# A long-convolution transform factored 64x64 in place of 256x16, with 32x64 and 64x32 array tiles in its first and last stage

## Chip, cores and metric

The kernel runs on one core of one Trainium2 chip. The metric is device time in microseconds (us) of one execution. A stage time is read from a single execution, and one difference of less than about 6 us in it is not firm. An execution of more than 1.5% above the fastest of its kernel is called slow and is left out of ratios. Where a profile is quoted, it is one execution, and its span is about 2 us shorter than the time that goes with it.

## The reference, cut to what matters

```python
def _A_ref(q, k, v, shift_k, ssm_k, ssm_D):        # H3: S = 2048 rows, D = 1024 channels
    k_shift = sum(k_pad[:, t:t+S, :] * shift_k[:, ks-1-t] for t in range(4))
    kv = k_shift * v
    y = irfft(rfft(kv, 2*S) * rfft(ssm_k, 2*S))[:S]  # causal convolution of length 4096
    return q * (y + kv * ssm_D)
def _B_ref(x, Lambda, B, C, log_dt, Dskip):         # S5: complex diagonal scan along S
    ...                                             # cut
    return 2 * Re(C h) + x * Dskip
return concatenate([a, b], axis=-1)                 # bfloat16, 2048 x 2048
```

Half A is the part that the change touches. One warning for what follows: evaluated on its inputs, the reference has values of about 3.8e-7 rms in half A and 2.5e-3 rms in half B. The comparison of outputs therefore does not see half A at all.

## The kernel before

Half A is a discrete Fourier transform of 4096 points, cut into factors, in three stages with scratch in DRAM between them. Stage 1 loads k and v, forms kv, transforms along the partitions and stores `Ys_kv` and `Ys_h`. Stage 2 loads those, multiplies the spectra, transforms back along the other factor and stores `Vs`. Stage 3 loads `Vs` as `vv`, does the last transform, multiplies by q and stores. Half B, in 16 chunks, runs beside all three, and a planner fixes one order of instructions for each engine.

```python
N1, N2, NFFT = 256, 16, 4096
kr = k.rearrange("(n s) d -> n s d", s=N2)           # vr, qr, oar alike: row t = 16*p + s
...
def k_(r):
    t_ = st["kring"][:, (r + 3) % c["kr"], :]        # a ring of buffers
    eng = spd if r > 0 else gpd                      # SyncE's hardware queue / GpSimd's queue
    if r >= 0:
        eng(t_, kr[:, r, :])                         # 128 partitions, 2 KB each
...
def am(n2, w):                                       # stage 1: 4 matmuls of 128x128 per n2
    cc, dh = divmod(w, 2)
    st["pa", n2, w] = ptile("ps_a", [P, 512])
    nc.tensor.matmul(st["pa", n2, w][:], F1t[:, cc, :], st["kv", n2][:, dh * 512:(dh + 1) * 512], start=True, stop=True)
...
E["ast"] = lambda n2, w: gpd(Ys_kv[w, n2, :, :], st.pop(("ysb", n2, w))[:])
...
def vl(n2):                                          # stage 3
    st["vv", n2] = atile("a3", "vv", [P, 2, D])
    for cc in range(2):
        spd(st["vv", n2][:, cc, :], Vs[cc, n2, :, :])
def ql(n2):
    st["qt", n2] = atile("a3", "qt", [P, D])
    spd(st["qt", n2][:], qr[:, n2, :])
def a3_(n2, w):
    ...
    for cc in range(2):
        nc.tensor.matmul(pt[:], Gt[:, cc, :], st["vv", n2][:, cc, w * 512:(w + 1) * 512], start=(cc == 0), stop=(cc == 1))
...
E["ost"] = lambda n2: gpd(oar[:, n2, :], st.pop(("ot", n2))[:])
```

## Time and profile before

The time is 401.72 us, the median of 3 runs (401.33 to 404.17). The stages end where the next one's first load is issued, which makes a table:

| border, before | us from the start |
|---|---|
| last k load issued | 125.2 |
| first l2h load issued (stage 1 ends) | 176.3 |
| first vv load issued (stage 2 ends) | 339.2 |
| end | 401.5 |

So the stages take 176.3, 162.9 and 62.3 us. The borders come from the views of single tiles. A line of such a view gives the issuing line, the engine, the output and input, the count, the shortest, median and longest issue in ns, and the time of the first and last issue:

```profile
L664 SPq DMA_DIRECT2D kring<-in_A_k_dram x15: 328/437/4037, 9.4 to 125.2; - x15
L764 SPq DMA_DIRECT2D l2h<-Ys_h x16: 339/498/1605, 176.3 to 305.2; - x16
```

The page's rows of 40 slices (one slice is 10 us here) show where the transfers were dense; a digit is the mean busy share of 16 DMA engines in tenths:

```profile
DMA  6999799698888463468599994998698553999982
GB/s 181 278 270 303 254 309 326 194 358 308 284 287 234 137 221 97 157 175 327 133 318 289 326 293 61 305 320 282 214 335 270 185 145 144 338 368 330 335 282 106
```

Until 130 us and again from 340 us most slices stand at 8 or 9 (10 of 13, and 5 of 6).

### The profile page before, as it was taken

To read this page: it belongs to the slowest core of one execution; us is meant where nothing else is said; L and a number is where in the kernel's file an instruction comes from. 1 tells how busy PE (TensorE), PEld (TensorE's weight loads), DVE (VectorE), ACT (ScalarE), POOL (GpSimd) and SP (SyncE) were. 2 spreads that over 40 slices of the span, in tenths; PEclk is the share of its full clock that TensorE was granted. 3 is DMA by queue.
4 is the path that set the end of the run, shared out by engine and by line. 5 is a ranking of instruction groups with operands and counts; after the bars stand their busy time and mean duration, and the time that the engine had idled before them with its cause. 6 is when DMAs were issued, how large, how long until landed. Compare 5 with 4: busy or idle time off the path is not lost.

```text
span 401.5 us, 9098 instructions
## 1 busy us (share of the span) xinstructions
PE 366.2 (91%) x3593; PEld 248.6 (62%) x3593; DVE 336.4 (84%) x338; ACT 291.6 (73%) x527; POOL 132.1 (33%) x228
## 2 busy tenths in 40 slices
PE   3589989998999999896989999798999999999994
PEld 0489988977668778582544465563655457667441
DVE  7695589998799999999779999984969894969861
ACT  6598989999797887642778976588778883453542
POOL 7002243435465564511333332224222431021121
PEclk9999999999999999998999999999999999999998
DMA  6999799698888463468599994998698553999982
GB/s 181 278 270 303 254 309 326 194 358 308 284 287 234 137 221 97 157 175 327 133 318 289 326 293 61 305 320 282 214 335 270 185 145 144 338 368 330 335 282 106
DMA packets 55132, 101.15 MB, mean 252 GB/s; under 512 B 23204, under 2 KB 25252, under 8 KB 55089
## 3 DMA queue, kind: packets, MB, share of 16 engines
q1 hardware_dynamic: 40864, 57.17, 47.3%
q0 software_dynamic: 14224, 43.40, 31.2%
q8 instruction: 28, 0.46, 0.5%
q14 instruction: 16, 0.12, 0.1%
HBM read 54.41 MB, written 33.55 MB: 219 GB/s over the span
## 4 chain that ended last, share of the span: by engine, by line
PE 42%; DMA 15%; issue 14%; DVE 13%; ACT 9%; POOL 4%; SPq 2%; POOLq 0%; ACTq 0%; DVEq 0%
PE ps_y L641 14%; PE ps_u L588 12%; PE ps_a L805 5%; PE ps_a L772 5%; DMA wts<-a_c_W 4%; DMA hab<-hab 3%; DVE h L618 3%; DMA Ys_kv<-ysb 3%; DVE hab L796 2%; DMA Ys_h<-ysbh 2%; DMA ld<-in_B_B_re_dram 2%; ACT ysbh L750 2%; POOL out_dram L850 2%; PE ps_a L698 1%; POOL Ys_h L757 1%
## 5 line engine op out<-in xcount | busy, mean ns | idle before, releaser
L641 PE MATMUL ps_y<-CT,h 128*128 128x512 bf16 x512 | 138.1, 381 | 3.6 <-ACT yo L656 1.6
L588 PEld LDWEIGHTS <-BT 128*128 128x128 bf16 x2048 | 120.8, 99 | 9.0 <-issue 1.5
L588 PE MATMUL ps_u<-xT,BT 128*128 128x128 bf16 x2048 | 126.0, 221 | 0.1
L641 PEld LDWEIGHTS <-h 128*128 128x128 bf16 x512 | 47.0, 98 | 50.8 <-DVE h L630 2.5
L618 DVE TENSOR_TENSOR_SCAN h<-rtab,h 128x1024 bf16<-128x1024 f32 x32 | 71.5, 2276 | 0.3
L590 ACT CAST u<-ps_u 128x512 bf16<-128x512 f32 x64 | 37.9, 604 | 41.9 <-PE ps_u L588 41.8
L757 POOL DMA_DIRECT2D Ys_h<-ysbh x64 | 46.2, 724 | 38.8 <-ACT ysbh L750 38.7
L796 DVE TENSOR_TENSOR hab<-x,hab 128x2048 bf16<-128x2048 bf16 x32 | 38.5, 1221 | 14.8 <-ACT hab L779 6.5
L600 DVE TENSOR_TENSOR mt<-u,Z 128x4096 bf16<-128x4096 bf16 x16 | 36.6, 2289 | 11.2 <-ACT u L590 11.0
L779 ACT CAST hab<-ps_a 128x512 bf16<-128x512 f32 x64 | 36.2, 600 | 10.8 <-DMA l2h<-Ys_h 5.7
L790 POOL DMA_DIRECT2D hab<-hab x32 | 16.8, 526 | 76.3 <-ACT hab L779 64.7
L817 ACT CAST vsb<-ps_a 128x512 bf16<-128x512 f32 x64 | 34.7, 596 | 9.7 <-PE ps_a L805 6.2
L785 ACT CAST x<-ps_a 128x512 bf16<-128x512 f32 x64 | 36.9, 599 | 5.2 <-PE ps_a L772 5.0
L750 ACT CAST ysbh<-ps_a 128x512 bf16<-128x512 f32 x64 | 36.8, 637 | 4.3 <-DMA Ys_h<-ysbh 2.6
L707 ACT CAST ysb<-ps_a 128x512 bf16<-128x512 f32 x64 | 36.0, 629 | 5.2 <-DMA Ys_kv<-ysb 1.6
L805 PE MATMUL ps_a<-hab,wts 128*128 128x512 bf16 x128 | 33.5, 380 | 4.0 <-DVE hab L796 3.2
L600 DVE TENSOR_TENSOR mt<-h,Z 128x4096 bf16<-128x4096 bf16 x16 | 36.5, 2283 | 0.0
L709 POOL DMA_DIRECT2D Ys_kv<-ysb x32 | 17.9, 559 | 53.4 <-ACT ysb L707 53.3
L681 DVE TENSOR_TENSOR mt<-kring,wbc 128x4096 bf16<-128x4096 bf16 (+3 forms) x16 | 30.2, 1886 | 0.1
L553 PE MATMUL ps_t<-ident,ld 128*128 128x128 bf16 x256 | 21.1, 233 | 9.2 <-DMA ld<-in_B_B_re_dram 5.8
L646 PE MATMUL ps_y<-Dd,xT 128*128 128x128 bf16 x128 | 28.0, 219 | 0.0
L772 PE MATMUL ps_a<-l2h,wts 128*128 128x512 bf16 x64 | 21.9, 386 | 5.6 <-DMA wts<-a_c_W 5.4
(117 smaller groups left out, 473.4 us busy)
## 6 DMA issues: line engine op xcount, KB each, us to landing
Ys_kv<-ysb POOLq DMA_DIRECT2D x32, 256.0 KB, 3.8
Ys_h<-ysbh POOLq DMA_DIRECT2D x64, 128.0 KB, 3.3
l2h<-Ys_h SPq DMA_DIRECT2D x16, 512.0 KB, 5.9
l2k<-Ys_kv SPq DMA_DIRECT2D x16, 512.0 KB, 8.2
hab<-hab POOLq DMA_DIRECT2D x64, 128.0 KB, 4.1
Vs<-vsb POOLq DMA_DIRECT2D x16, 512.0 KB, 7.2
vv<-Vs SPq DMA_DIRECT2D x32, 256.0 KB, 5.0
hk<-in_A_ssm_k_dram SPq DMA_DIRECT2D x8, 512.0 KB, 7.2
```

The source lines that it names most:

```text
L588: nc.tensor.matmul(pu[:, w, jl, :], BT[:, 2 * jp + jl, w, d, :], xT[:, d, :], start=(d == 0), stop=(d == ND - 1))
L590: E["ue"] = lambda i, jp: nc.scalar.copy(st["u", i][:, :, 2 * jp:2 * jp + 2, :], st.pop(("pu", i, jp))[:])
L600: nc.vector.tensor_mul(m, s_, win(Z))
L618: nc.vector.tensor_tensor_scan(gf[:, a * W:(a + 1) * W], rt1, gf[:, a * W:(a + 1) * W], 0.0, ALU.mult, ALU.add)
L641: nc.tensor.matmul(py[:], h[:, 1 - w, j, :], CT[:, j, w, dh * 512:(dh + 1) * 512], start=(j == 0 and w == 0), stop=(j == NJ - 1 and w == 1))
L750: nc.scalar.copy(st["yh", qd, n4, w // 2][:, :, w % 2, :], st.pop(("pa", qd, n4, w))[:].rearrange("p (c d) -> p c d", c=2))
L757: gpd(Ys_h[cc, n0:n0 + 2, :, qd * DQ:(qd + 1) * DQ].rearrange("n k d -> k n d"), t_[:, cc, :, :])
L772: nc.tensor.matmul(st["ps", nm, g, w][:], st["w", gq][:, gi, 0, :], st[nm, gq][:, gi, w * 512:(w + 1) * 512], start=True, stop=True)
L779: nc.scalar.copy(st["hab", g][:, 0, w * 512:(w + 1) * 512], st.pop(("ps", "l2h", g, w))[:])
L785: nc.scalar.copy(st["x16", g][:, w * 512:(w + 1) * 512], st.pop(("ps", "l2k", g, w))[:])
L796: nc.vector.tensor_mul(hab[:], st.pop(("x16", g))[:].unsqueeze(1).to_broadcast([P, 2, D]), hab[:])
L805: nc.tensor.matmul(pt[:], st["w", gq][:, gi, 1 + a, :], hab[:, a, w * 512:(w + 1) * 512], start=(a == 0), stop=(a == 1))
```

## The change

The intent is cheaper matrix work. With 64x64 factors, the first and last transforms contract over 32 and 64 rows only, so TensorE's array can be used as several small tiles side by side. To put four groups of 32 rows onto the partitions, the sequence is read in another order: row t is 64n + 16q + r, and partition 32q + n gets it. The diff, cut to its core:

```diff
-N1, N2, NFFT = 256, 16, 4096
+N1, N2, NFFT = 64, 64, 4096
...
-    kr = k.rearrange("(n s) d -> n s d", s=N2)
...                                                   (v, q and out_a alike)
+    kr, vr, qr, oar = (a.rearrange("(n q s) d -> q n s d", q=4, s=NR) for a in (k, v, q, out_a))
...
-            eng(t_, kr[:, r, :])
+            eng(t_, kr[:, :, r, :])
...
-        cc, dh = divmod(w, 2)
-        nc.tensor.matmul(..., F1t[:, cc, :], st["kv", n2][:, dh * 512:(dh + 1) * 512], start=True, stop=True)
+        b = 32 * w
+        for dh in range(2):
+            nc.tensor.matmul(pt[64 * dh:64 * dh + 64, :], F1t[b:b + 32, :], st["kv", n2][b:b + 32, dh * 512:(dh + 1) * 512], start=True, stop=True)
...
-    E["ast"] = lambda n2, w: gpd(Ys_kv[w, n2, :, :], st.pop(("ysb", n2, w))[:])
+        for dh in range(2):
+            gpd(Ys_kv[n2, 2 * w:2 * w + 2, :, dh * 512:(dh + 1) * 512].rearrange("q k d -> k q d"), t_[64 * dh:64 * dh + 64, :, :])
...
-        for cc in range(2):
-            spd(st["vv", n2][:, cc, :], Vs[cc, n2, :, :])
+        for dh in range(2):
+            spd(st["vv", n2][64 * dh:64 * dh + 64, :, :], Vs[n2, :, :, dh * 512:(dh + 1) * 512].rearrange("q k d -> k q d"))
...
-        spd(st["qt", n2][:], qr[:, n2, :])
+        spd(st["qt", n2][:], qr[:, :, n2, :])
...
-        for cc in range(2):
-            nc.tensor.matmul(pt[:], Gt[:, cc, :], st["vv", n2][:, cc, w * 512:(w + 1) * 512], start=(cc == 0), stop=(cc == 1))
+        for qt in range(4):
+            nc.tensor.matmul(pt[32 * qt:32 * qt + 32, :], Gt[64 * w:64 * w + 64, :], st["vv", n2][64 * w:64 * w + 64, qt, :],
+                             start=True, stop=True, tile_position=(64 * w, 32 * qt))
...
-    E["ost"] = lambda n2: gpd(oar[:, n2, :], st.pop(("ot", n2))[:])
+    E["ost"] = lambda n2: gpd(oar[:, :, n2, :], st.pop(("ot", n2))[:])
```

In what follows, a "narrow" transfer is one whose DRAM side is [4, 32, 1024], and a "wide" one has at least 32 rows as its slowest dimension.

More of the change, by code (lines that the diff above doesn't have):

```diff
@@ L20 @@
 TWO_PI = 2.0 * math.pi
-N1, N2, NFFT = 256, 16, 4096
+N1, N2, NFFT = 64, 64, 4096
 NG = 32
+NR = 16
 def a_constants():
-    n1 = np.arange(128)[:, None]; k1 = np.arange(128)[None, :]
+    n1 = np.arange(32)[:, None]; k1 = np.arange(NG)[None, :]
     ang = 2 * np.pi * n1 * (k1 + 0.5) / N1
-    F1 = np.stack([np.cos(ang), -np.sin(ang)], axis=1)
-    G = np.stack([np.cos(ang.T) * 2 / NFFT, -np.sin(ang.T) * 2 / NFFT], axis=1)
-    s = np.arange(4)[:, None, None, None]; g = np.arange(NG)[None, :, None, None]
-    n2 = np.arange(N2)[None, None, :, None]; k2 = np.arange(N2)[None, None, None, :]
-    kk1 = 32 * s + g
-    phi = 2 * np.pi * n2 * (2 * kk1 + 1 + 2 * N1 * k2) / (2 * NFFT)
-    cph, sph = np.cos(phi), np.sin(phi)
-    W2 = np.zeros((2, 4, N2, NG, 2, 4, N2))
-    Wa = np.zeros((2, 4, N2, NG, 2, 4, N2))
-    Wb = np.zeros((2, 4, N2, NG, 2, 4, N2))
-    for si in range(4):
-        c_ = cph[si]; s_ = sph[si]
-        c_n2k2 = np.transpose(c_, (1, 0, 2)); s_n2k2 = np.transpose(s_, (1, 0, 2))
-        W2[0, si, :, :, 0, si, :] = c_n2k2
-        W2[1, si, :, :, 0, si, :] = s_n2k2
-        W2[0, si, :, :, 1, si, :] = -s_n2k2
-        W2[1, si, :, :, 1, si, :] = c_n2k2
-        c_k2n2 = np.transpose(c_, (2, 0, 1)); s_k2n2 = np.transpose(s_, (2, 0, 1))
-        Wa[0, si, :, :, 0, si, :] = c_k2n2
-        Wa[0, si, :, :, 1, si, :] = s_k2n2
-        Wa[1, si, :, :, 0, si, :] = -c_k2n2
-        Wa[1, si, :, :, 1, si, :] = -s_k2n2
-        Wb[0, si, :, :, 0, si, :] = -s_k2n2
-        Wb[0, si, :, :, 1, si, :] = c_k2n2
-        Wb[1, si, :, :, 0, si, :] = -s_k2n2
-        Wb[1, si, :, :, 1, si, :] = c_k2n2
-    f = lambda a: np.ascontiguousarray(a.reshape(128, -1), dtype=np.float32).astype(ml_dtypes.bfloat16)
-    W2 = np.transpose(W2, (0, 2, 1, 3, 4, 5, 6))
-    Wa = np.transpose(Wa, (0, 1, 2, 3, 4, 6, 5))
-    Wb = np.transpose(Wb, (0, 1, 2, 3, 4, 6, 5))
-    W3 = np.stack([W2.reshape(128, NG, 128), Wa.reshape(128, NG, 128), Wb.reshape(128, NG, 128)], axis=2)
-    return f(F1), f(G), f(W3)
@@ new lines, in a_constants @@
+    f1 = np.stack([np.cos(ang), -np.sin(ang)], axis=1).reshape(32, 64)
+    F1 = np.tile(f1, (4, 1))
+    F1h = np.zeros((32, 4, 2, 2, 64))
+    for qt in range(4):
+        F1h[:, qt, qt // 2, qt % 2, :] = f1
+    G = np.tile(np.concatenate([np.cos(ang.T), -np.sin(ang.T)], axis=0) * 2 / NFFT, (2, 1))
+    r = np.arange(NR)[:, None]; qt = np.arange(4)[None, :]
+    n2 = (16 * qt + r).reshape(-1)[:, None, None]
+    g = np.arange(NG)[None, :, None]
+    k2 = np.arange(N2)[None, None, :]
+    phi = 2 * np.pi * n2 * (2 * g + 1 + 2 * N1 * k2) / (2 * NFFT)
@@ new lines, in a_constants @@
+    co, si = np.cos(phi), np.sin(phi)
+    W2 = np.stack([np.stack([co, -si], axis=2), np.stack([si, co], axis=2)], axis=1)
+    cT, sT = (np.transpose(a, (2, 1, 0)) for a in (co, si))
+    Wa = np.stack([np.stack([cT, sT], axis=3), np.stack([-cT, -sT], axis=3)], axis=0)
+    Wb = np.stack([np.stack([-sT, cT], axis=3), np.stack([-sT, cT], axis=3)], axis=0)
+    f = lambda a: np.ascontiguousarray(a.reshape(128, -1), dtype=np.float32).astype(ml_dtypes.bfloat16)
+    W3 = np.stack([a.reshape(128, NG, 128) for a in (W2, Wa, Wb)], axis=2)
@@ L63 @@
+    return f(F1), f(F1h), f(G), f(W3)
 class Task:
@@ L344, in full_kernel @@
     Dd = const.tile([P, ND, P], BF16, name="Dd")
-    F1n, Gn, W3n = a_constants()
+    F1n, Fhn, Gn, W3n = a_constants()
     F1d = nc.inline_tensor(F1n, name="a_c_F1")
+    Fhd = nc.inline_tensor(Fhn, name="a_c_Fh")
     Gd = nc.inline_tensor(Gn, name="a_c_G")
     W3d = nc.inline_tensor(W3n, name="a_c_W3")
-    F1t = const.tile([P, 2, P], BF16, name="F1t")
-    Gt = const.tile([P, 2, P], BF16, name="Gt")
+    F1t = const.tile([P, 64], BF16, name="F1t")
+    Fht = const.tile([P, 2, P], BF16, name="Fht")
+    Gt = const.tile([P, 32], BF16, name="Gt")
     W3v = W3d.ap().rearrange("p (g t m) -> p g t m", g=NG, t=3)
-    Ys_kv = tc.dram_tile([2, N2, P, D], BF16, name="Ys_kv")
-    Ys_h = tc.dram_tile([2, N2, P, D], BF16, name="Ys_h")
-    Vs = tc.dram_tile([2, N2, P, D], BF16, name="Vs")
-    kr = k.rearrange("(n s) d -> n s d", s=N2)
-    vr = v.rearrange("(n s) d -> n s d", s=N2)
-    qr = q.rearrange("(n s) d -> n s d", s=N2)
-    oar = out_a.rearrange("(n s) d -> n s d", s=N2)
+    Ys_kv = tc.dram_tile([NR, 4, 64, D], BF16, name="Ys_kv")
+    Ys_h = tc.dram_tile([NR, 4, 64, D], BF16, name="Ys_h")
+    Vs = tc.dram_tile([NR, 4, 64, D], BF16, name="Vs")
+    kr, vr, qr, oar = (a.rearrange("(n q s) d -> q n s d", q=4, s=NR) for a in (k, v, q, out_a))
     Bv = (B_Bre.rearrange("(j i) d -> i j d", i=P), B_Bim.rearrange("(j i) d -> i j d", i=P))
@@ L528, in full_kernel, with ld_F @@
     E["ld_w"] = ld_w
-    E["ld_F"] = lambda: gpd(F1t[:].rearrange("p c k -> p (c k)"), F1d.ap())
-    E["ld_G"] = lambda: gpd(Gt[:].rearrange("p c k -> p (c k)"), Gd.ap())
+    def ld_F():
+        gpd(F1t[:], F1d.ap())
+        gpd(Fht[:].rearrange("p c k -> p (c k)"), Fhd.ap())
+    E["ld_F"] = ld_F
+    E["ld_G"] = lambda: gpd(Gt[:], Gd.ap())
     def ld_sd():
@@ L663, in k_ @@
         if r >= 0:
-            eng(t_, kr[:, r, :])
+            eng(t_, kr[:, :, r, :])
         else:
-            eng(t_[1:113, :], kr[0:112, N2 + r, :])
-            eng(t_[113:P, :], kr[112:P - 1, N2 + r, :])
+            eng(t_[1:32, :], kr[3, 0:31, NR + r, :])
+            eng(t_[32:P, :], kr[0:3, :, NR + r, :])
     E["k"] = k_
@@ L671, in v_ @@
         st["v", n2] = ldt()
-        (spd if n2 else gpd)(st["v", n2][:], vr[:, n2, :])
+        (spd if n2 else gpd)(st["v", n2][:], vr[:, :, n2, :])
     E["v"] = v_
@@ L695, in am @@
     def am(n2, w):
-        cc, dh = divmod(w, 2)
-        st["pa", n2, w] = ptile("ps_a", [P, 512])
-        nc.tensor.matmul(st["pa", n2, w][:], F1t[:, cc, :], st["kv", n2][:, dh * 512:(dh + 1) * 512], start=True, stop=True)
+        pt = ptile("ps_a", [P, 512])
+        st["pa", n2, w] = pt
+        b = 32 * w
+        for dh in range(2):
+            nc.tensor.matmul(pt[64 * dh:64 * dh + 64, :], F1t[b:b + 32, :], st["kv", n2][b:b + 32, dh * 512:(dh + 1) * 512], start=True, stop=True)
         if w == 3:
@@ L703, in ae, with ast @@
     def ae(n2, w):
-        cc, dh = divmod(w, 2)
-        if dh == 0:
-            st["ysb", n2, cc] = atile("a1", "ysb", [P, D])
-        nc.scalar.copy(st["ysb", n2, cc][:, dh * 512:(dh + 1) * 512], st.pop(("pa", n2, w))[:])
+        if w % 2 == 0:
+            st["ysb", n2, w // 2] = atile("a1", "ysb", [P, 2, 512])
+        nc.scalar.copy(st["ysb", n2, w // 2][:, w % 2, :], st.pop(("pa", n2, w))[:])
     E["ae"] = ae
-    E["ast"] = lambda n2, w: gpd(Ys_kv[w, n2, :, :], st.pop(("ysb", n2, w))[:])
+    def ast(n2, w):
+        t_ = st.pop(("ysb", n2, w))
+        for dh in range(2):
+            gpd(Ys_kv[n2, 2 * w:2 * w + 2, :, dh * 512:(dh + 1) * 512].rearrange("q k d -> k q d"), t_[64 * dh:64 * dh + 64, :, :])
+    E["ast"] = ast
     def hl(qd, m):
@@ L719, in hT @@
         for m in range(2):
-            hv = st["hk", qd, m][:].rearrange("p (n s) -> p s n", s=N2)
+            hv = st["hk", qd, m][:].rearrange("p (n s) -> p s n", s=NR)
             for n in range(4):
@@ L741, in hm @@
         for cc in range(2):
-            nc.tensor.matmul(pt[:, cc * DQ:(cc + 1) * DQ], F1t[:, cc, :], st["hT", qd, n4][:, w, :], start=True, stop=True)
+            nc.tensor.matmul(pt[:, cc * DQ:(cc + 1) * DQ], Fht[:, cc, :], st["hT", qd, n4][:, w, :], start=True, stop=True)
         if w == 3:
@@ L756, in hst @@
         for cc in range(2):
-            gpd(Ys_h[cc, n0:n0 + 2, :, qd * DQ:(qd + 1) * DQ].rearrange("n k d -> k n d"), t_[:, cc, :, :])
+            gpd(Ys_h[n0:n0 + 2, 2 * cc:2 * cc + 2, :, qd * DQ:(qd + 1) * DQ].rearrange("n q k d -> (q k) n d"), t_[:, cc, :, :])
     E["hst"] = hst
@@ L763, in l_ @@
             st[nm, gq] = a2.tile([P, GC, D], BF16, name=nm, bufs=c["l2"])
-            spd(st[nm, gq][:], Ys.rearrange("c n (s g) d -> (c n s) g d", g=NG)[:, gq * GC:(gq + 1) * GC, :])
+            spd(st[nm, gq][:], Ys.rearrange("r q (c g) d -> (r q c) g d", g=NG)[:, gq * GC:(gq + 1) * GC, :])
         st["w", gq] = a2.tile([P, GC, 3, P], BF16, name="wts", bufs=c["l2"])
@@ L818, in full_kernel @@
     E["sae"] = sae
-    E["vst"] = lambda gq: gpd(Vs.rearrange("c n (s g) d -> (c n s) g d", g=NG)[:, gq * GC:(gq + 1) * GC, :], st.pop(("vsb", gq))[:])
+    E["vst"] = lambda gq: gpd(Vs.rearrange("r q (c g) d -> (r q c) g d", g=NG)[:, gq * GC:(gq + 1) * GC, :], st.pop(("vsb", gq))[:])
     def vl(n2):
-        st["vv", n2] = atile("a3", "vv", [P, 2, D])
-        for cc in range(2):
-            spd(st["vv", n2][:, cc, :], Vs[cc, n2, :, :])
+        st["vv", n2] = atile("a3", "vv", [P, 4, 512])
+        for dh in range(2):
+            spd(st["vv", n2][64 * dh:64 * dh + 64, :, :], Vs[n2, :, :, dh * 512:(dh + 1) * 512].rearrange("q k d -> k q d"))
     E["vl"] = vl
@@ L834, in a3_ @@
         st["po", n2, w] = pt
-        for cc in range(2):
-            nc.tensor.matmul(pt[:], Gt[:, cc, :], st["vv", n2][:, cc, w * 512:(w + 1) * 512], start=(cc == 0), stop=(cc == 1))
+        for qt in range(4):
+            nc.tensor.matmul(pt[32 * qt:32 * qt + 32, :], Gt[64 * w:64 * w + 64, :], st["vv", n2][64 * w:64 * w + 64, qt, :],
+                             start=True, stop=True, tile_position=(64 * w, 32 * qt))
         if w == 1:
```

## The prediction

> **What bounds the kernel now.** I began with the busy shares of the page. No engine is alone: TensorE's records cover 91% of the span, VectorE's 84%, ScalarE's 73%, and records of pipelined matmuls overlap. So I cut the span where the kernel's own stages end. The first loads of stage 2 (l2h) are issued at 176 us, because they need every store of stage 1; the first loads of stage 3 (vv) at 339 us, because they need every store of stage 2. The second half of the kernel, an SSM scan in 16 chunks, runs beside all three stages in one fixed order per engine. The view by stretches, asked at these borders (each cell is busy us and, in brackets, instructions; the last three columns are the granted TensorE clock, the mean busy share of the 16 DMA engines, and GB/s):
>
> ```profile
> 0.00:130.00 130.00, 113.14 (x1451) 94.43 (x1452) 109.23 (x150) 112.24 (x189) 50.78 (x84) 1.00 0.89 275
> 130.00:172.00 42.00, 40.61 (x449) 30.16 (x447) 40.90 (x37) 33.39 (x62) 22.57 (x34) 1.00 0.47 151
> 172.00:339.00 167.00, 156.31 (x1244) 90.76 (x1242) 142.05 (x113) 119.52 (x230) 47.88 (x90) 0.99 0.78 246
> 339.00:402.00 63.00, 56.13 (x461) 33.28 (x458) 44.21 (x41) 26.47 (x48) 10.82 (x20) 0.97 0.81 284
> ```
>
> To see: until 130 us the DMA engines are 89% busy, so stage 1 is nearly as full of transfers as of TensorE work; from 130 to 172 us they have slack. Stage 3 shows 0.81 over the whole, and asked in slices of 10 us it is full:
>
> ```profile
> 345.00:355.00 10.00, 10.00 (x80) 5.76 (x77) 6.94 (x8) 5.08 (x9) 2.17 (x4) 1.00 1.00 365
> 355.00:365.00 10.00, 10.00 (x102) 6.69 (x99) 9.08 (x7) 4.88 (x9) 1.08 (x2) 1.00 1.02 364
> 365.00:375.00 10.00, 10.00 (x99) 6.58 (x98) 8.03 (x10) 5.60 (x11) 1.66 (x4) 1.00 0.98 331
> 375.00:385.00 10.00, 9.76 (x52) 4.62 (x51) 9.93 (x9) 3.82 (x8) 2.12 (x4) 1.00 0.97 336
> ```
>
> Stage 3 is bound by DMA; the instructions only follow the landings. Then I read the groups that the change touches, and the DMA issues (size, median us from issue to landing):
>
> ```profile
> L698 PE MATMUL ps_a<-acc,F1t 128*128 128x512 bf16 x64 | 20.3, 379 | 0.6 <-DVE acc L691 0.3 <-ACT ysbh L750 0.3
> L836 PE MATMUL ps_a<-vv,Gt 128*128 128x512 bf16 x64 | 17.2, 379 | 0.0
> ```
>
> ```profile
> q1 hardware_dynamic: 40864, 57.17, 47.3%
> ...
> Ys_kv<-ysb POOLq DMA_DIRECT2D x32, 256.0 KB, 3.8
> ...
> vv<-Vs SPq DMA_DIRECT2D x32, 256.0 KB, 5.0
> ...
> qt<-in_A_q_dram SPq DMA_DIRECT2D x16, 256.0 KB, 5.1
> ...
> kring<-in_A_k_dram SPq DMA_DIRECT2D x15, 256.0 KB, 4.5
> ld<-in_A_v_dram SPq DMA_DIRECT2D x15, 256.0 KB, 3.6
> ```
>
> The matmuls that the change makes cheaper are 64 and 64 of 3593. In the chain of waits a run of six L836 matmuls takes 1.29 us, 0.215 us each, so together they fill 128 x 0.215 = 27.5 us of TensorE. The loads in the second list are what the change reshapes as a side effect.
>
> **What the Trainium skill says.** (1) "DMA: Bandwidth & Descriptors", section "Why a DMA increments its semaphore by 16 and not by 1": a copy runs on k of the 16 engines, k being the largest number up to 16 that divides the size of the slowest dimension that isn't 1 on both sides; on the hardware queue the engines are the lowest-numbered k, and only these post a completion. The trace agrees where it can: the four parameter loads of 8 partitions, the first transfers of SyncE, left 32 packets of 256 B and 32 completion packets of 4 B on the hardware queue, 8 each and not 16. (2) Same page, "Rules for kernel authors": an outermost dimension below 16 confines the whole DMA to at most so many engines. No load of this size in the kernel before has one, so its time is not shown yet. (3) "TensorEngine Tiling (Array Packing)", "Key Properties": a change of tiling mode drains TensorE. (4) "TensorE: Matmul & The Clock Gate", Part 3, "Measured speedup vs the span model": four row tiles of K=32, N=512 run 3.07 times as fast. The kernel before has no tiled matmul, so neither (3) nor (4) is shown.
>
> **The change part by part.** I compared the instruction orders of the two builds: the scheduler's plan is untouched, and apart from the items below every engine does the same things in the same order.
>
> *TensorE.* Stage 1: 64 matmuls of 128x128 weights become 128 of 32x64, in pairs with one row group and two column groups. If only the pair overlaps, the time stays 64 x 0.215 = 13.8 us; if neighbouring row groups overlap too, it could fall to a quarter where 6 or 8 stand together; in most places just 2 stand between full-array matmuls, with a drain at each side. I take 0 to -5 us. Stage 3: 64 become 128 of 64x32, four column tiles side by side: 32 x 0.215 = 6.9 us in place of 13.8. In stage 1 DMA sets most of the pace and in stage 3 all of it, so of these 7 to 12 us I count 2 on the path.
>
> *Stores and vv.* The kv stores become 64 of 128 KB in place of 32 of 256 KB: 32 more issues x 0.555 us (their median) = 18 us of GpSimd, which is busy 73 of the first 172 us; hidden. The vv loads have 1 KB runs, so 8192 packets in place of 4096. The trace's packets have medians of 18 ns (256 B), 65 ns (1536 B) and 84 ns (2048 B) on this queue; on the line between the first two 1 KB is 46 to 47 ns, an estimate. 8192 x 47 / 16 less 4096 x 84 / 16 = +2.5 us of every DMA engine in stage 3.
>
> *k, v and q loads: the main item.* Row t of the sequence is now n*64 + q*16 + s, so the DRAM side of each load is [4, 32, 1024], where it was [128, 1024]; the partition side is 128. By (1), k = 4 for the 15 k, 15 v and 16 q loads on the hardware queue, always the same four engines. These have to carry 64 KB of each load, 32 packets, where they carried 8.
> Stage 1: 30 loads x 128 packets of 2 KB at a mean of 101 ns in this stage (84 uncrowded) = 388 us of engine time, 24.2 us on each of 16, 97.0 on each of 4 (80.6 at 84 ns). All transfers until 172 us are 0.89 x 130 + 0.47 x 42 = 135.4 us per engine. The four then need 135.4 - 24.2 + 80.6 to 97.0 = 192 to 208 us; if everything else becomes uncrowded too (x 0.88) some 180. With about 10 us of unfilled time at start and end that is 190 to 218, where the border is at 176: +14 to +42, I take +28. It can't hide: the B and C weights, the x transposes and the Ys stores need a sixteenth from each of the four engines as well, so they queue behind.
> Stage 3: 16 x 128 packets at 96 ns = 12.3 us per engine, on four 49.2 (43.0 at 84 ns). All transfers are 0.81 x 63 = 51.0, so the four need 51.0 - 12.3 + 2.5 + 43.0 to 49.2 = 84 to 90, or about 80 if the rest speeds up. The stretch of 63 us has 12 unfilled: 92 to 102, so +29 to +39; I take +32.
> The output stores get the same [4, 32] shape, but on GpSimd's queue; the same section (1) has the engines of such a queue taken in rotation, so on average they are even, and I count 0. Stage 2 has the same transfers as before: 0.
>
> Sum: 401.7 + 28 + 32 - 2 = 460 us.
>
> **The rivals.** *Loads still spread over 16 engines* (a 128-partition destination may be enough): then only the tiles and packets count, -7 to +5, so 395 to 407. For it: the partition side has 128 rows; against: the 8 and not 16 completions of the small loads. *The tiles are the gain that was meant*: TensorE is 91% busy, and if matmuls bound stage 1 up to 17 us would go, some 385 us. Against it: the full DMA slices of stage 3, and 0.89 until 130 us. *Worse than counted*: output stores kept to the same four engines add 1024 packets of 4 KB x 160 ns x (1/4 - 1/16) = 31 us in stage 3, some 490 us. *Better than counted*: loads run up to 35 us ahead of their use (the last k load is issued at 125 us, its last multiply starts at 164), so stage 1 may lose only 10 us: some 440.
>
> **Range and chances.** I give the four-engine reading 85%, for the rule is stated for this queue and the one small case agrees. Within it the ends 428 and 492 come from +10 and +24 in the two stages, and from +42 and +48. Most of the other 15% is within 2%. So 0.03 faster, 0.12 the same, 0.85 slower.
>
> **What will show it.** If k is 4, each of 46 loads posts 4 completions, not 16: the hardware queue's packets go from 40864 to 40864 + 4096 - 46 x 12 = 44408; with 16 engines, to 44960. The mean DMA share in stage 3 should then fall to about 0.55 while the stage gets longer (four engines full, twelve waiting), qt and vv should take 8 us or more to land, and the first l2h issue should move to about 205 us. Stage 2 should keep its 163 us. If it stretches, if packets number 44960, or if TensorE's time in L698's successor rises by over 10 us, a step above is wrong.

## More of the kernel before

The start of SyncE's own queue matters later; columns are start, duration, queue and line, operation, how many:

```profile
14.55 0.35 SPq L713 DMA_DIRECT2D hk<-in_A_ssm_k_dram  x1
15.50 0.33 SPq L664 DMA_DIRECT2D kring<-in_A_k_dram  x1
16.24 6.27 SPq L576 DMA_TRANSPOSE xT<-in_B_x_dram  x2
```

An issue is over in a third of a microsecond; two transposes of x take 6.27 us together.

## The result

The changed kernel takes 491.61 us (median of 4 runs, 489.76 to 495.27); the kernel before took 402.92 us beside it (4 runs, 401.33 to 404.17). The ratio is 1.221, with a 95% interval of 1.214 to 1.229. Ratios here are the mean time of one kernel's fast runs over the mean of the other's fast runs of the same rounds, so they are not quite the ratio of the medians. The direction was right; the size was not: some 89 us were lost where I had said 58, and 491.61 stands at the very end of my range (428 to 492).

| us | before | after | difference | predicted |
|---|---|---|---|---|
| last k load issued at | 125.2 | 167.0 | +41.8 | |
| stage 1 | 176.3 | 226.4 | +50.1 | +28 |
| stage 2 | 162.9 | 155.8 | -7.1 | 0 |
| stage 3 | 62.3 | 107.3 | +45.0 | +32 |

The borders again, in the changed kernel:

```profile
L655 SPq DMA_DIRECT2D kring<-in_A_k_dram x15: 523/697/4945, 8.9 to 167.0; - x15
L761 SPq DMA_DIRECT2D l2h<-Ys_h x16: 348/471/1005, 226.4 to 348.0; - x16
L821 SPq DMA_DIRECT2D vv<-Vs x32: 573/988/4892, 382.2 to 459.3; - x32
```

And the stretches between them, with the columns of the prediction's first view (us, then busy us of PE, PEld, DVE, ACT and POOL, granted clock, DMA share, GB/s):

```profile
0.00:172.00 172.00, 122.52 (x1427) 95.29 (x1428) 110.07 (x150) 110.97 (x184) 63.23 (x103) 0.90 0.83 199
172.00:226.00 54.00, 50.29 (x579) 35.68 (x577) 47.12 (x42) 36.96 (x68) 31.97 (x49) 0.97 0.56 160
226.00:382.00 156.00, 151.05 (x1194) 87.42 (x1192) 135.20 (x107) 118.41 (x228) 47.22 (x89) 1.00 0.80 258
382.00:490.00 108.00, 67.67 (x533) 33.84 (x530) 45.36 (x41) 25.89 (x48) 13.57 (x20) 0.76 0.63 167
```

Stage 3 carries the same bytes, at 167 GB/s where it was 284, and its mean DMA share falls from 0.81 to 0.63 while it gets longer. More idle engines and a longer stage at once is what a few overloaded engines among sixteen look like. The packet records of the trace (start, duration and size of each) say it directly: the q loads are the only 2 KB packets of the hardware queue in stage 3, and more than four of them were under way at once for only 3 of its 107 us. In split_all (below), where the q loads are not narrow, it was 20 of 75 us. In the first 172 us the rate is 199 GB/s, after 275 in the first 130 of before. Between them, from 172 to 226 us, there is slack again (0.56), as there was from 130 to 172: that stretch has moved back by some 40 us as a block and has grown longer.

The packets of the hardware queue show how many engines took part:

```profile
q1 hardware_dynamic: 44408, 57.17, 45.1%
```

That is the number that I had worked out for 4 completions in place of 16 for each of 46 loads. The rows of 40 slices (12 us each now) show the damage at the two ends:

```profile
PEclk9976899899987999999999999999999957797595
DMA  7998747677896866456899939978853857776742
GB/s 183 139 106 214 253 140 243 217 231 255 271 142 216 169 206 164 158 133 204 278 314 300 339 116 307 345 253 257 304 167 112 195 141 211 188 199 177 208 139 71
```

106 GB/s in the third slice, and no slice of the last nine above 211. The granted clock dips to 5 to 7 tenths in several slices of stage 3: TensorE is busy 68 of 108 us there. I read the clock as a companion of the waiting, not as a cause, because the waits name transfers. Two of the longest waits for a transfer in stage 3 (engine, line, releaser: us in total, times, longest):

```profile
DVE ot L846 <- DMA qt<-in_A_q_dram: 32.5, 9, 7.7
PE ps_a L833 <- DMA vv<-Vs: 25.3, 8, 6.8
```

The chain that ended last says the same of its first half (start, length, what):

```profile
387.63 19.04 DMA qt<-in_A_q_dram
...
406.73 11.18 DMA qt<-in_A_q_dram
```

The chain puts 30 of the first 36 us of the stage down to two waits for q loads. From 419 us on it names only GpSimd's output stores, with gaps of up to 7 us that it puts down to no wait. The page gives no landing for the loads of this queue any more, so such waits are what is left to read.

SyncE's queue shows a second effect:

```profile
8.86 8.52 SPq L655 DMA_DIRECT2D kring<-in_A_k_dram  x3
17.51 3.26 SPq L710 DMA_DIRECT2D hk<-in_A_ssm_k_dram  x1
20.82 3.92 SPq L655 DMA_DIRECT2D kring<-in_A_k_dram  x1
24.78 16.20 SPq L567 DMA_TRANSPOSE xT<-in_B_x_dram  x2
```

Issues that took a third of a microsecond stand for 3 to 4 us, and two transposes of x take 16.20 us where they took 6.27. SyncE issues in order, so each stand also delays all loads after it, wide ones too.

The matmuls that were to gain (line, engine, tile, out<-in, count, busy us, mean ns, idle before and its releasers):

```profile
L691 PE MATMUL ps_a<-acc,F1t 32*64 32x512 bf16 x128 | 17.2, 422 | 1.5 <-ACT ysbh L747 1.5
L833 PE MATMUL ps_a<-vv,Gt 64*32 64x512 bf16 x128 | 12.6, 454 | 25.9 <-DMA vv<-Vs 25.3 <-ACT yo L647 0.6
```

They fell from 20.3 to 17.2 us and from 17.2 to 12.6 us of busy time, and the second group waits 25.9 us for its operand.

### The profile page after: what moved, and what is told of

It is laid out like the page before. It is cut to its first block, busy times and chain, and to the rows that moved or that the text cites. A ratio compares the mean times of both kernels' runs of the same rounds, so it can differ in the third digit from the quotient of the medians.

```text
span 489.5 us, 9405 instructions
## 1 busy us (share of the span) xinstructions
PE 391.5 (80%) x3721; PEld 252.2 (52%) x3721; DVE 337.8 (69%) x338; ACT 292.2 (60%) x527; POOL 156.0 (32%) x261
## 3 DMA queue, kind: packets, MB, share of 16 engines
q1 hardware_dynamic: 44408, 57.17, 45.1%
## 4 chain that ended last, share of the span: by engine, by line
PE 16%; issue 14%; DMA 12%; DVE 6%; POOL 3%; ACT 2%; SPq 1%; POOLq 0%; DVEq 0%; ACTq 0%
PE ps_y L632 7%; DMA qt<-in_A_q_dram 6%; DMA hab<-hab 5%; PE ps_u L579 3%; PE ps_a L769 3%; PE ps_a L802 3%; DVE hab L793 2%; DVE h L609 2%; POOL out_dram L848 2%; DVE mt L591 1%; ACT hab L776 1%; SPq L821 1%; ACT vsb L814 1%; DMA Vs<-vsb 1%; POOL hab L787 1%
## 5 line engine op out<-in xcount | busy, mean ns | idle before, releaser
L632 PE MATMUL ps_y<-CT,h 128*128 128x512 bf16 x512 | 149.4, 405 | 1.9 <-ACT yo L647 1.8
L579 PE MATMUL ps_u<-xT,BT 128*128 128x128 bf16 x2048 | 132.5, 226 | 2.0 <-DMA xT<-in_B_x_dram 2.0
L579 PEld LDWEIGHTS <-BT 128*128 128x128 bf16 x2048 | 125.9, 102 | 12.0 <-issue 4.1
L632 PEld LDWEIGHTS <-h 128*128 128x128 bf16 x512 | 48.0, 102 | 57.1 <-issue 18.2
L705 POOL DMA_DIRECT2D Ys_kv<-ysb x64 | 38.5, 607 | 72.6 <-ACT ysb L699 70.2
L846 DVE TENSOR_TENSOR ot<-ot,qt 128x1024 bf16<-128x1024 bf16 x16 | 11.0, 690 | 45.8 <-DMA qt<-in_A_q_dram 32.5
L544 PE MATMUL ps_t<-ident,ld 128*128 128x128 bf16 x256 | 22.4, 240 | 23.6 <-DMA ld<-in_B_B_re_dram 8.2
L747 ACT CAST ysbh<-ps_a 128x512 bf16<-128x512 f32 x64 | 35.8, 605 | 7.8 <-DMA Ys_h<-ysbh 6.5
L848 POOL DMA_DIRECT2D out_dram<-ot x16 | 11.2, 702 | 79.3 <-DVE ot L846 73.2
L833 PE MATMUL ps_a<-vv,Gt 64*32 64x512 bf16 x128 | 12.6, 454 | 25.9 <-DMA vv<-Vs 25.3
```

The source lines that it names most:

```text
L579: nc.tensor.matmul(pu[:, w, jl, :], BT[:, 2 * jp + jl, w, d, :], xT[:, d, :], start=(d == 0), stop=(d == ND - 1))
L632: nc.tensor.matmul(py[:], h[:, 1 - w, j, :], CT[:, j, w, dh * 512:(dh + 1) * 512], start=(j == 0 and w == 0), stop=(j == NJ - 1 and w == 1))
L705: gpd(Ys_kv[n2, 2 * w:2 * w + 2, :, dh * 512:(dh + 1) * 512].rearrange("q k d -> k q d"), t_[64 * dh:64 * dh + 64, :, :])
```

## The experiments

Fifteen kernels ran, in four calls; each call had its own runs of the kernel before on the same chip (medians 403.81, 403.37, 402.65 and 400.42 us), and the ratios refer to those. My theory, after the packet counts, was that the shape of the narrow transfers makes the whole loss. The rivals were that the tiles and their half-width transfers make a good part of it, that the new order of rows is slow in DRAM whatever the shape, and that SyncE's queue standing still, rather than four full engines, is the loss. Where an expectation has letters, they name readings. Stage times come from each kernel's profiled run, read at the same borders as above.

| kernel | us | ratio (95%) | last k issue | stage 1 | stage 2 | stage 3 |
|---|---|---|---|---|---|---|
| before | 402.92 | 1 | 125.2 | 176.3 | 162.9 | 62.3 |
| after | 491.61 | 1.221 (1.214 to 1.229) | 167.0 | 226.4 | 155.8 | 107.3 |
| no_tiles | 404.39 | 1.001 (0.995 to 1.007) | 127.1 | 179.2 | 162.5 | 63.0 |
| order_alone | 489.18 | 1.212 (1.203 to 1.222) | 169.5 | 228.4 | 157.2 | 96.8 |
| split_all | 424.78 | 1.051 (1.043 to 1.059) | 134.5 | 188.0 | 160.2 | 74.6 |
| split_v | 477.93 | 1.182 (1.168 to 1.196) | 148.7 | 210.5 | 157.1 | 105.3 |
| split_k | 475.90 | 1.187 (1.168 to 1.207) | 147.6 | 206.8 | 155.1 | 109.9 |
| split_start | 483.28 | 1.199 (1.191 to 1.207) | 155.4 | 216.6 | 154.7 | 111.0 |
| split_q | 487.32 | 1.209 (1.200 to 1.218) | 166.9 | 228.6 | 155.0 | 100.3 |
| split_out | 487.24 | 1.209 (1.200 to 1.218) | 169.2 | 228.9 | 155.1 | 100.1 |
| split_qo | 458.20 | 1.143 (1.130 to 1.156) | 167.5 | 225.9 | 156.3 | 74.1 |
| deep_a3 | 496.38 | 1.231 (1.222 to 1.241) | 167.3 | 227.0 | 156.8 | 109.4 |
| tiles_natural | 416.89 | 1.035 (1.027 to 1.043) | 125.2 | 182.5 | 156.9 | 74.9 |
| vv_1k128 | 409.66 | 1.018 (1.011 to 1.025) | 124.6 | 180.2 | 156.8 | 65.7 |
| vv_2k128 | 407.61 | 1.009 (1.002 to 1.015) | 133.5 (slow run) | 189.4 (slow run) | 156.6 (slow run) | 64.5 (slow run) |
| kvq_gpsimd | 479.64 | 1.190 (1.178 to 1.201) | 177.6 | 229.7 | 157.1 | 88.1 |
| natural_gpsimd | 423.16 | 1.056 (1.044 to 1.068) | 141.6 | 194.8 | 157.4 | 69.5 |

One run of order_alone, two of vv_1k128 and the profiled one of vv_2k128 were slow; medians contain them, ratios do not. vv_1k128's verdict is unclear at 2%; no_tiles and vv_2k128 are the same as before within 2%, all others slower.

**no_tiles and order_alone: the order without the tiles, and the reverse.** no_tiles keeps the 64x64 factors, but with full 128x128 matmuls (zeros in the weights), the natural row order and wide transfers. order_alone is the kernel before with nothing changed but the order of rows; its constants are permuted to match (so one more constant is loaded at the start, and the last transform's is loaded when stage 3 begins).

```diff
# no_tiles, against after
-    kr, vr, qr, oar = (a.rearrange("(n q s) d -> q n s d", q=4, s=NR) for a in (k, v, q, out_a))
+    kr, vr, qr, oar = (a.rearrange("(n s) d -> n s d", s=NR) for a in (k, v, q, out_a))
+    # am and a3_ as in before with zero-padded Fht and Gt; ysb stored and vv loaded as 128 rows of 2 KB
# order_alone, against before
-    kr = k.rearrange("(n s) d -> n s d", s=N2)
+    kr = k.rearrange("(n q s) d -> q n s d", q=4, s=N2)      # v, q, out_a alike; eng(t_, kr[:, :, r, :]) and so on
+    # rows of F1 and columns of G permuted by 4n + q
```

> The 64x64 factorization with full 128x128 matmuls (zero-padded first- and last-stage matrices) and the row order of the kernel before, so every load and store has one outer dimension of 128 again. If the [4, 32] shape of the loads is the whole cost: 398 to 408 us, first stage-2 load near 176 us, first stage-3 load near 339, 40,864 packets on the hardware queue. If the factorization itself or its scratch layout costs: over 430 us.

> The kernel before, still 256x16 and without array tiles, with only the row order of the change: k, v, q loads and output stores in the shape [4, 32], first- and last-stage matrices permuted to match, so the result stays right. If the shape is the whole cost: 480 to 492 us, first stage-2 load at about 226 us, 40,864 - 46 x 12 = 40,312 packets on the hardware queue. If array tiles, 1 KB runs or more stores carry a large part: under 450 us.

The factorization by itself costs nothing measurable: 404.39 us, with an interval for the ratio that has 1 in it. The order of the rows, with the old matmuls, gives 489.18 us, nearly the whole loss. Its packets on the hardware queue:

```profile
q1 hardware_dynamic: 40312, 57.17, 45.4%
```

This is 40864 - 46 x 12, so here too each of 46 loads posted 4 completions and not 16. Its stage 3 is 96.8 us and not 107.3, a difference of about the size that the vv loads cost below.

**split_all: all four quarters as transfers of their own.** The tiles, the order of rows and the bytes stay; each narrow transfer becomes four of 32 rows.

```diff
-            eng(t_, kr[:, :, r, :])
+            for b in range(4):
+                eng(t_[32 * b:32 * b + 32, :], kr[b, :, r, :])
# v, q and output stores alike
```

> The changed kernel with every k, v and q load and every output store of this half issued as four transfers of 32 rows, so each can use 16 engines; tiles, 1 KB runs and kv stores stay. If the shape is the cost: 395 to 415 us. If tiles, mode changes or 1 KB runs are: over 450 us.

It ran in 424.78 us, between the two ranges, so 67 of the 89 us came back although the same rows go to the same partitions, with four times as many issues. The packets agree with 16 completions for each quarter (40864 + 4096 + 46 x 3 x 16 = 47168):

```profile
q1 hardware_dynamic: 47168, 57.18, 48.6%
```

It is the shape of the access pattern and not the order of rows that costs. Some 20 us remain; they are in stage 1 (188.0 for 176.3) and stage 3 (74.6 for 62.3).

**tiles_natural, vv_1k128 and vv_2k128: the tiles with wide transfers.** These three give wrong values in half A: they keep the tiled matmuls but load rows in the natural order. The first has the change's vv loads, in two halves of 64 partitions; the others bring the same bytes onto 128 partitions, in runs of 1 KB and of 2 KB.

```diff
# tiles_natural, against after
-    kr, vr, qr, oar = (a.rearrange("(n q s) d -> q n s d", q=4, s=NR) for a in (k, v, q, out_a))
+    kr, vr, qr, oar = (a.rearrange("(n s) d -> n s d", s=NR) for a in (k, v, q, out_a))
# vv_1k128, against tiles_natural
-        for dh in range(2):
-            spd(st["vv", n2][64 * dh:64 * dh + 64, :, :], Vs[n2, :, :, dh * 512:(dh + 1) * 512].rearrange("q k d -> k q d"))
+        R = Vs[n2, :, :, :].rearrange("q k d -> (q k) d")
+        for cc in range(2):
+            spd(st["vv", n2][:, cc::2, :], R[128 * cc:128 * cc + 128, :].rearrange("p (a d) -> p a d", a=2))
# vv_2k128: [:, 2 * cc:2 * cc + 2, :] in place of [:, cc::2, :]
```

> The changed kernel with array tiles, 1 KB runs and 64 kv stores kept, but k, v, q and the output in the row order of the kernel before, so every transfer is again one of 128 outer rows. The result is wrong on purpose (rows reach the wrong tile); the work is the same. If the load shape is the whole cost: 395 to 408 us, and any gain of the tiles shows as less than 404. If tiles, 1 KB runs or more stores cost too, as split_all's 424.8 may mean: 412 to 425.

> tiles_natural (wide loads, result wrong on purpose), where stage 3 took 74.8 us against 63.0 without tiles, with the vv loads still in runs of 1 KB but onto all 128 partitions in each transfer, not 64. If the half of the partitions was the cost: stage 3 at 63 to 66, total 402 to 408. If the 1 KB runs were: stage 3 stays at 72 to 76, total 412 to 420.

> tiles_natural with vv loaded as in the kernel before, runs of 2 KB onto 128 partitions; the array tiles stay (result wrong on purpose). If vv's shape is what the tiles' layout costs in stage 3: 63 to 66 there, total 400 to 408. If the tiled matmuls themselves are: 72 to 76, total 412 to 420.

With all else wide, vv in halves makes stage 3 74.9 us; on 128 partitions with the same 1 KB runs it is 65.7 us, and with 2 KB runs 64.5 us. So 9.2 us belong to the halves, 1.2 to the shorter runs, and at most 1.5 (64.5 for no_tiles' 63.0) to the tiled matmuls; the last two are rough, as the profiled run of vv_2k128 was a slow one. The DMA issues of tiles_natural (KB, median us from issue to landing):

```profile
vv<-Vs SPq DMA_DIRECT2D x32, 256.0 KB, 9.1
...
qt<-in_A_q_dram SPq DMA_DIRECT2D x16, 256.0 KB, 9.1
```

and of vv_1k128:

```profile
vv<-Vs SPq DMA_DIRECT2D x32, 256.0 KB, 5.5
...
qt<-in_A_q_dram SPq DMA_DIRECT2D x16, 256.0 KB, 5.3
```

Both have 8192 packets of 1 KB on the hardware queue in stage 3. In tiles_natural they have a median of 71 ns, in vv_1k128 46 ns, which is what I had estimated; together 574 and 405 us, a difference of 169 / 16 = 10.6 us of every engine, about the 9.2 us. Why a packet to one half of the partitions takes longer isn't shown. Nor does it always look like this: in split_all the same halves have a median of 46 ns, 506 us together, and land in 4.8 us, so how much of its stage 3 the halves cost and how much the many more issues isn't separated. vv_2k128, in which only the tiles and the kv stores are left of the change, has a ratio of 1.009 (1.002 to 1.015): even freed of all else, the tiles gave no gain. Its last transform is busy 9.6 us where before it was 17.2, and the time doesn't follow:

```profile
L834 PE MATMUL ps_a<-vv,Gt 64*32 64x512 bf16 x128 | 9.6, 385 | 0.0
```

**split_q, split_out, split_qo and deep_a3: stage 3.** split_q makes the q loads wide and leaves the output stores narrow, split_out the reverse, split_qo both. deep_a3 keeps all narrow and gives stage 3 more buffers.

```diff
# split_q (split_out: the same of E["ost"]; split_qo: both)
-        spd(st["qt", n2][:], qr[:, :, n2, :])
+        for b in range(4):
+            spd(st["qt", n2][32 * b:32 * b + 32, :], qr[b, :, n2, :])
# deep_a3
-  vv=4, qt=4, ot=3
+  vv=6, qt=8, ot=6
```

> The changed kernel with only the q loads split in four. Stage 1 keeps its first stage-2 load at about 226 us. If the q loads alone make stage 3 long: it falls from 107 to 65 to 75 us, total 448 to 458. If the output stores of shape [4, 32] have a large part: stage 3 stays over 85 us.

> The changed kernel with only the output stores split in four; k, v and q loads stay narrow. split_q showed a stage 3 of 100 us with narrow stores alone. If the narrow q loads alone are as bad as I predicted: stage 3 at 85 to 95 us. If the stores were nearly all of it: under 82. First stage-2 load near 226 us in both; total 457 to 477.

> The changed kernel with q loads and output stores both split in four; k and v stay narrow. Narrow q alone (split_out) and narrow stores alone (split_q) each left stage 3 at 100 us, both together at 107, none at 74.6 (split_all). If stage 3 depends on its own transfers alone: 73 to 77 us here, first stage-2 load at 226 to 229, total 456 to 464. If stage 1 leaves something behind for stage 3: over 80 there.

> The changed kernel with deeper buffers in stage 3: 6 vv, 8 q and 6 output tiles for 4, 4 and 3. The four engines' own need there is 80 to 90 us of the 107. If buffers run out while transfers queue up: stage 3 falls to 88 to 96 us, total 470 to 480. If the four engines are simply full, or the issuing queue is what stands: no change, 485 to 495.

From 107.3 us of stage 3, widening q takes 7.0 us, widening the stores 7.2 us, widening both 33.2 us. Counted from the wide end: q narrow alone adds 25.5 us (split_out less split_all), stores narrow alone 25.7 us (split_q less split_all), both 32.7 us. They are two limits side by side: either one that is left nearly sets the stage, and the second adds only 7 us. split_out's 100.1 us lies above both its ranges. The stretch of stage 3 in split_q:

```profile
384.00:484.00 100.00, 61.02 (x515) 32.67 (x521) 44.73 (x41) 25.88 (x48) 13.55 (x20) 0.80 0.67 179
```

in split_out:

```profile
384.00:484.00 100.00, 65.08 (x521) 33.41 (x527) 45.22 (x41) 25.99 (x48) 33.79 (x68) 0.78 0.66 180
```

and in split_qo:

```profile
382.00:456.00 74.00, 56.75 (x526) 31.24 (x531) 45.23 (x41) 25.81 (x48) 33.64 (x68) 0.95 0.84 244
```

With one narrow kind of transfer left, whichever of the two, the DMA share is 0.66 to 0.67 and the rate 179 to 180 GB/s; without any it is 0.84 and 244, and the clock is back at 0.95. In split_out, where q alone is narrow, exactly four packets (of 64 bytes and more) were under way on all queues together for 20.7 of the 100 us (before: 0.4 of 62): four engines at work, twelve idle. That split_qo reaches 74.1 us although its first 226 us are as slow as after's also shows that stage 3 depends on its own transfers alone. More buffers did nothing (496.38 us, stage 3 109.4), so neither limit is a lack of buffers in this stage. What a narrow store waits for is not shown. That it runs on four engines has a sign: GpSimd's queue in the changed kernel has 4080 packets of 8 bytes that the kernel before has none of. That is 16 x 12 for each of its 18 transfers of [4, 32] and 16 x 13 for each of the three k loads of [3, 32], so 16 for every engine left out. The same count fits kvq_gpsimd (below) to the packet: 64 x 192 + 3 x 208 = 12912.

**split_v, split_k and split_start: stage 1.** Each makes a part of stage 1's narrow loads wide and leaves the rest: all v, all k, or only the first k rows (up to row 4) and the first v.

```diff
# split_v (split_k: the same in k_; split_start: in k_ for r <= 4 and in v_ for n2 == 0)
-        (spd if n2 else gpd)(st["v", n2][:], vr[:, :, n2, :])
+        for b in range(4):
+            (spd if n2 else gpd)(st["v", n2][32 * b:32 * b + 32, :], vr[b, :, n2, :])
```

> The changed kernel with only the v loads split in four, so that half of stage 1's load on the four engines is gone. Theory A (the four engines set the time until the last load has landed, and after it the fixed order still needs the 46 to 54 us it had): need until the last load 115.7 - 24.2 + 12.1 + 40.3 = 144 us, so the first stage-2 load at 190 to 198 us, total 455 to 465. Theory B (as predicted: the four engines' work of the whole stage, free to fill the slack after 130 us): 135.4 - 24.2 + 12.1 + 40 to 48 + 10 = 174 to 182 us, total 440 to 450.

> The changed kernel with only the k loads split in four; v and q loads and the stores stay narrow. With all wide the first stage-2 load is at 182.5 us (188.0 when split in four), with all narrow at 226.4; v alone wide gave 210.5, so about 16 of the 44 us; the loads of the start alone 10. If the parts add up, k alone wide gives 196 to 203 us, total 467 to 475. If whichever narrow stream is left keeps the whole stand: over 208.

> The changed kernel with only the first k and v loads (rows up to 4, and the first v) split in four. The trace of the changed kernel shows SyncE held 12.6 us at the third x transpose while the four engines work off the first k loads. If this stand at the start adds to stage 1: first stage-2 load at 205 to 214 us, not 226, total 472 to 480. If the later loads make up for it because the four engines are full anyway: 222 to 228, total 486 to 493.

split_v was sent to choose between two readings of stage 1, the prediction's and one in which the loads gate the stage, and its 210.5 us lies above the ranges of both; the gated reading is nearer. split_k, sent with the expectation that the parts add up, came at 206.8, above the 196 to 203 that this gave. Alone, k wide takes off 19.6 us, v wide 15.9 and the start 9.8, of 226.4; all of it wide (split_all) takes 38.4. The borders of split_k:

```profile
L763 SPq DMA_DIRECT2D l2h<-Ys_h x16: 354/508/881, 206.8 to 327.4; - x16
L656 SPq DMA_DIRECT2D kring<-in_A_k_dram x60: 310/419/2320, 8.3 to 147.6; - x60
```

The last k load is issued at 147.6 us, midway between before's 125.2 and after's 167.0, and stage 1 ends 59.2 us later. I come back to this below.

**kvq_gpsimd and natural_gpsimd: narrow on another queue.** Is it SyncE's queue standing still, or narrowness itself? kvq_gpsimd is the changed kernel with k, v and q issued from GpSimd. Its control natural_gpsimd has the same queue and wide loads (wrong in half A, as tiles_natural).

```diff
# kvq_gpsimd against after, natural_gpsimd against tiles_natural (v and q alike)
-        eng = spd if r > 0 else gpd
+        eng = gpd
```

> The changed kernel with all k, v and q loads issued by GpSimd in place of SyncE, same shape, so still four engines each but, by the rotation of that queue, not always the same four, and SyncE's queue never stands behind them. If the pile-up on the same four is the cost: 405 to 435 us. If it is that each transfer is narrow and lands late: over 465.

> The control for kvq_gpsimd: k, v and q loads issued by GpSimd, but in wide shape (row order of the kernel before, result wrong on purpose; tiles kept). kvq_gpsimd took 479.6 us, with the first stage-2 load at 229.7. If a narrow transfer harms on whatever engines it falls: 182 to 190 us there and 412 to 425 in all. If moving the loads into GpSimd's queue is itself what kept kvq_gpsimd slow: 215 or more, over 450 in all.

Narrow loads on GpSimd's queue give 479.64 us, wide ones 423.16 us. Narrowness costs 34.9 us in stage 1 (229.7 less 194.8) and 18.6 us in stage 3 (88.1 less 69.5) on this queue too. It is less than the 43.9 and 32.4 us on SyncE's queue (after less tiles_natural), so some, not most, of the loss hangs on the hardware queue. By its expectation, 479.64 us (over 465) speaks for narrowness on whatever engines, and against a pile-up on always the same four. Moving wide loads to GpSimd costs 12.3 us in stage 1 by itself (194.8 less 182.5). And the transposes still stand in kvq_gpsimd, though no k or v load is in their queue:

```profile
12.95 16.71 SPq L567 DMA_TRANSPOSE xT<-in_B_x_dram  x2
30.33 12.96 SPq L567 DMA_TRANSPOSE xT<-in_B_x_dram  x1
```

and in its control natural_gpsimd they stand less:

```profile
13.79 11.73 SPq L567 DMA_TRANSPOSE xT<-in_B_x_dram  x2
26.26 1.23 SPq L567 DMA_TRANSPOSE xT<-in_B_x_dram  x1
```

So a transpose can be held up by narrow transfers of another queue, too.

No record of these traces names the engine, but the packets show that on this queue it is not always the same four. In stage 3 of kvq_gpsimd more than six of the queue's 4 KB packets were under way at once for 41 of 88 us; leaving out the 14 us after each store of half B, which is wide, it is 11 of 29 us, with up to 16. Nor do engines idle there. The stretch of stage 3 in kvq_gpsimd and in natural_gpsimd:

```profile
386.70:474.90 88.20, 61.20 (x515) 30.84 (x520) 44.71 (x41) 26.27 (x48) 24.50 (x36) 0.86 0.92 204
352.20:421.70 69.50, 55.96 (x513) 29.60 (x519) 44.33 (x41) 26.36 (x48) 19.33 (x36) 0.93 0.90 258
```

The DMA share is 0.92 and 0.90, where after's was 0.63. So the packets themselves took longer: 0.92 x 88.2 less 0.90 x 69.5 is 18.6 us of every engine, all that narrowness costs there. Narrow transfers lose in two ways, then: four engines overloaded on SyncE's queue, slower packets on GpSimd's. Why the packets are slower isn't shown.

## Why the prediction was wrong

**Right.** The cause I named, narrow loads, is the cause. *The main item* said that the reshaped loads run on 4 engines, and three packet counts fit that to the packet (44408, 40312 and, for quarters on 16, 47168); the packets under way in stage 3 fit it too. Making only that shape wide brings back 67 of 89 us. That it is *always the same four* is only a part of the cost: on GpSimd's queue, where it isn't, narrowness costs 56.5 us (kvq_gpsimd less natural_gpsimd), on SyncE's 74.7 (after less tiles_natural). *TensorE* was right in kind: the tiles' gain is not on the path. The kv stores' 32 more issues stayed hidden as far as no_tiles against vv_2k128 can tell.

**Wrong: stage 1's step "the four then need 192 to 208 us", +28, measured +50.** The failing term is the 135.4 us of all transfers until 172 us, to which I compared the end of the stage. It lets the four engines' backlog be worked off in the slack from 130 to 172 us. But no k or v load is issued in that stretch: the last k load must be reached first, and the fixed order then still has some 50 us of work (51.1 us before). So the sum belongs to the end of the loads: 0.89 x 130 = 115.7 us of all engines, less 24.2, plus 80.6 = 172 us on the four; half of it narrow gives 115.7 - 12.1 + 40.3 = 144. These are estimates made after the fact, at the uncrowded 84 ns; they meet the last k issue at 167.0 and 169.5 (after, order_alone) and at 148.7 and 147.6 us (split_v, split_k). The rest follows whole: +41.8 of the +50.1 us is there at the last k load. The other 8.3 us are no loss but a border that moved, for stage 2 is shorter by 7.1 (below). The stands of SyncE's queue at the start are a part of the 41.8: without them (split_start) the last k load comes 11.6 us earlier. How the rest divides between the stands and the four engines' sum the runs don't settle: with the loads off SyncE's queue (kvq_gpsimd) narrowness still costs 34.9 us of stage 1, but there the transposes still stand and it is not always the same four engines, so this confirms neither.

**Wrong: stage 3's +32, measured +45.** Three of its terms can be read from the runs, going from before to after by way of split_all (74.6) and split_out (100.1); the order matters, as the last two limits overlap. *The vv loads, "+2.5 us"*: +12.3, with all that isn't narrow in it (+12.6 in tiles_natural, where nothing is split in four). I counted the shorter runs (measured at 1.2) and not the halves (9.2); the small rest may be tiles or chance. *The q loads*: 25.5, where my sum leaves 32 - 2.5 = 29.5; mis-sized little. *Output stores, "in rotation, so on average they are even, and I count 0"*: +7.2 on top of q, and 25.7 when they alone are narrow. 12.3 + 25.5 + 7.2 = 45.0. The zero was the worst of the three, for anyone who had widened only the q loads would have got back 4 us of time and not 30. Its reason fails as well: in kvq_gpsimd the groups of engines do change, and narrow transfers still cost 18.6 us of stage 3.

**Wrong: stage 2's 0.** It became 7.1 us shorter; it is 162.5 in no_tiles and 154.7 to 160.2 in all others. But this is the same shift as the 8.3 us above. From the last k issue to the first vv issue before takes 213.9 us and after 215.2, and all fifteen kernels with these loads on SyncE's queue take 212 to 219. So the first two stages together lost 43.0 us, of which 41.8 are the last k load's. tiles_natural shows the shift alone: stage 1 +6.2, stage 2 -6.0, their sum and its last k load as before. What moves the border between them is open, but it costs nothing.

**The rivals.** *Loads still spread over 16 engines* and *the tiles are the gain* fell with the packet count and with vv_2k128. *Worse than counted* gave some 490 us, and the kernel took 491.6, but not by its working: it left stage 1 at +28 (measured +50) and put 31 us of stores on top of q's in stage 3 (measured 7). Two errors cancelled. *Better than counted* hoped that loads which run ahead would absorb the loss. The run-ahead itself was lost: the last k load moved by 41.8 us.

**The signs I had listed.** The first l2h issue was to be at about 205 us and came at 226.4. Stage 3's DMA share was to be 0.55 and is 0.63. vv and qt's landings aren't given, but the chain has single waits of 19.0 and 11.2 us for q. TensorE's time in L698's successor fell by 3.1 us.

**The range.** Its upper end took +42 and +48 for the two stages. Stage 3 stayed inside that and stage 1 went 8 us over it, which stage 2 gave back. The lower end was added up wrongly: +10 and +24 on 401.7 are 436 and not 428.

No variant beats the kernel before. no_tiles ties with it.

## What to carry to other kernels

Before changing the order of rows for the sake of the matrix engine, write down the access pattern of every load and store that follows from it, and look at its slowest dimension: here [4, 32, 1024] in place of [128, 1024] cost 67 us, and four transfers of 32 rows each in place of one gave them back (split_all). When transfers slow down in a stage with a fixed order, work out when the last load arrives and add what must still follow it; don't spread the work over the whole stage, for the slack behind the last load was of no use here. A saving on an engine that the path doesn't pass through, like 3 to 8 us of matmuls here, pays for nothing.

## What the Trainium skill lacked or had wrong

- "DMA: Bandwidth & Descriptors", section "Why a DMA increments its semaphore by 16 and not by 1": the number of engines is right for this case. Loads with [4, 32, 1024] on the DRAM side and 128 partitions on the other gave 44408 packets, which is 4 completions each, and quarters of 32 rows gave 47168, which is 16 each.
- The same section has an all-engine completion on GpSimd's queue and consecutive engines from a round-robin cursor. It doesn't say what a narrow store then costs. Here stage 3 took 100.3 us with only the stores narrow and 74.6 with none (split_q, split_all). I had read rotation as "even, so 0", and the number speaks against that reading. It doesn't mention the 8-byte packets that GpSimd's queue has with narrow transfers, either: 4080 in the changed kernel, none in before and split_all, a count that fits 16 for each engine left out.
- The same page, "Rules for kernel authors", says of two transfers to disjoint partition halves that they serialize, and advises one of 128 partitions. The advice is right: vv in two halves of 64 partitions made stage 3 9.2 us longer than the same bytes and runs on 128 (tiles_natural, vv_1k128).
- No page that I read says that the issue of a transpose stands while narrow loads are under way: two took 16.20 us where they had taken 6.27, and 16.71 us with the narrow loads on GpSimd's queue, where wide ones gave 11.73.
- "TensorE: Matmul & The Clock Gate", Part 3, "Measured speedup vs the span model", gives 3.07 for four row tiles. That case has no run here. The page has no figure for tiles in twos or fours between full-array matmuls: twice as many matmuls were busy for 17.2 us in place of 20.3 in stage 1 (32x64, in after) and for 9.6 in place of 17.2 in stage 3 (64x32, in vv_2k128, a slow run), and the time gained nothing.
